# K, V, dV and dK moved one DMA per head pair in key order, and weights transposed on TensorE, in a two-block attention kernel with backward

## The chip, the cores and the metric

The kernel runs on one core of one Trainium2 chip. The metric is the device time of one execution in microseconds (us), lower is better. Durations below come from one profiled execution of the kernel before the change.

## What is computed

Two independent attention blocks A and B, each with its own x, caches and weights, run forward, and then the gradients of all ten inputs are computed from `grad_out`. For one block (the sizes are those of the inputs):

```python
B, Sq, D = 8, 96, 640          # batch, queries, model width
H, Sk, Dh = 32, 512, 128       # heads, keys, head width
q = (x @ wq).reshape(B, Sq, H, Dh).transpose(0, 2, 1, 3)
scores = einsum("bhqd,bhkd->bhqk", q, k_cache) * Dh ** -0.5
p = softmax(scores)
o = einsum("bhqk,bhkd->bhqd", p, v_cache)
out = o.transpose(0, 2, 1, 3).reshape(B, Sq, H * Dh) @ wo
...
_out, _vjp = jax.vjp(_f, A_x, A_k_cache, ..., B_wo)   # all inputs
_grads = _vjp(grad_out)
```

All arrays are bf16. Per block the outputs are `out`, dx, dK, dV, dwq and dwo. Per head and batch entry, K, V, dK and dV are 512x128 each, so 128 KB.

## The kernel before

**Ticks.** Work is cut into pieces that an `Emitter` sorts by (tick, slot). One tick is one (head, batch) pair: 2 blocks x 32 heads x 8 batch entries = 512 ticks. Heads go in pairs (`HP = 2`), and ticks alternate between the two heads of a pair for one batch entry. `OFF` and `HK` say by how many ticks a stage stands before or after its own tick; `SLOTS` sorts the stages inside a tick. The order of instructions on each engine follows from this table, and within what it leaves open from the framework's scheduler; engines run their own list in order and wait for each other by semaphores.

**The stages of one tick.** `c_s2a`: S = Q K^T (PE, tile `S_ps`) and the row maximum `negm` (DVE). `c_s2b`: exp into `E_sb` with row sums (ACT). `c_s3a`, `c_s3b`: 1/rowsum `rinv` (DVE) and P = E * rinv into `P_sb` (POOL). `c_s45`: P transposed on PE, copied by ACT to `PT_sb`; one tick later O^T from `V_sb` and `PT_sb` (tile `optp_ps`, copied to `OT_h`). `c_s4`: dV = P^T dO (`dV_ps`), copied by ACT to `dV_sb` (L325) and stored (L326). `c_s5b`, `c_s6`: `prod` on POOL, dP = dO V^T (`dP_ps`), the row term `dl_ps`, and dS = (dP - dl) * P on DVE into `dS_sb` (L349). `c_s78`: dS transposed and, a tick later, dQ^T from `K_sb`. `c_s7`: dK (`dK_ps`), copied by ACT to `dK_sb` (L389) and stored (L390).

**Loads.** `p_ldT` reads K and V of two heads transposed, by one transposing DMA each per head pair, into `KT_p` and `VT_p` (L232, 5 buffers). `c_ldn` reads K and V as they lie, one DMA per head, into `K_sb` and `V_sb` (L241, 7 buffers). All of these, the dV and dK stores and the transposed weight loads are issued from one queue, SP's (in the trace SPq). SP issues in order, and an issue that must wait holds everything behind it. `dV_sb` and `dK_sb` have 3 buffers each: ACT may write a buffer again only when the store from three heads earlier has landed.

**Key order.** In the transposed tile the key index is split as key = (r, f, c) with 8 x 16 x 4 values, and r lies innermost in memory. S reads it in the order (c, f, r), runs of 8 adjacent bf16. So the columns of S, P, dP and dS stand in that permuted order, and the natural loads and the dV, dK stores go through `keys_in`, which puts key (r, f, c) on partition (f, r).

**Per head.** `pA` loads the weights of a head pair (`wq_p` from POOL's queue, `woT_p` by a transposing DMA on SP, L172). `pC` makes Q^T and dO^T (tile `q_ps`), `pD` their untransposed forms, `qA`, `qB`, `qD` the weight gradients. After every group of 4 heads, `gW` loads `wo_r` and, transposed by a DMA on SP, `wqT_r` (L454), and 36 pieces `gU` (L477, tile `o_ps`) add the group's part to the output and to dx.

All PSUM tiles share 8 banks that go round in the order of the program.

Of the kernel before, what the change touches and what calls it, by code (L numbers as in the profile page):

```python
# [56 lines left out]
def build_block(tc, em, tick0, blk, x, kc, vc, wq, wo, g_all, out_all, dx, dk, dv, dwq, dwo, ident, ones, pools, HG=4, first=True, groups=None):  # L57
# [108 lines left out]
    def pA(h):  # L166
        def f():
            wq_p = hd.tile([128, DC, HP * 128], BF16, name="wq_p", bufs=2)
            with nc.allow_non_contiguous_dma(reason="per-pair wq slice"):
                nc.gpsimd.dma_start(wq_p[:], wq_v[:, :, h * 128:(h + HP) * 128])  # L170
            woT_p = hd.tile([128, DC, HP * 128], BF16, name="woT_p", bufs=2)
            nc.sync.dma_start_transpose(woT_p[:], wo[h * 128:(h + HP) * 128, :])  # L172
# [12 lines left out]

    def pC(h, which, si):
        def f():
            st = HS[(blk, h)]
            (t0, w) = tsplits[si]
            if which == 0:  # L190
                dst = st["QT_h"]
                lhs = lambda c: st["wq_h"][:, c, :]
                rhsT = S["xT"]
                sc = scale
            else:
                dst = st["dOT_h"]
                lhs = lambda c: st["woT_h"][:, c, :]
                rhsT = S["gT"]
                sc = None
            q_ps = bank([128, w], F32, "q_ps")  # L200
            for c in range(DC):
                nc.tensor.matmul(q_ps[:], lhs(c), rhsT[:, c, t0:t0 + w], start=(c == 0), stop=(c == DC - 1))  # L202
            evac(EV["pC%d%d" % (which, si)], dst[:, t0:t0 + w], q_ps[:], sc)
        return f
# [19 lines left out]
    def keys_in(kv, h, b):  # L224
        return kv[b, h].rearrange("(r f c) d -> f r (c d)", r=R8, f=F4, c=KC)

    def p_ldT(h, b, which):
        def f():
            key = "KT" if which == 0 else "VT"
            t_ = kvp.tile([128, F4 * KC, 16], BF16, name=key + "_p", bufs=5)  # L230
            src = (kc if which == 0 else vc)[b, h:h + HP].rearrange("h (r f) d -> (h r) (f d)", r=R8)
            nc.sync.dma_start_transpose(t_[:], src)  # L232
            for j in range(HP):
                CS.setdefault((blk, h + j, b), {})[key] = t_[:, :, j * R8:(j + 1) * R8].rearrange("p (f c) r -> p c f r", c=KC)
        return f

    def c_ldn(h, b, which):
        def f():
            key = "K_sb" if which == 0 else "V_sb"
            t_ = kvp.tile([128, KC, 128], BF16, name=key, bufs=7)  # L240
            nc.sync.dma_start(t_[:].rearrange("p c d -> p (c d)"), keys_in(kc if which == 0 else vc, h, b))  # L241
            CS[(blk, h, b)][key] = t_
        return f
# [72 lines left out]
    def c_s4(h, b):  # L316
        def f():
            st = CS[(blk, h, b)]
            hs = HS[(blk, h)]
            P_sb = st["P_sb"]  # L320
            dV_ps = bank([128, KC * 128], F32, "dV_ps")
            for c in range(KC):
                nc.tensor.matmul(dV_ps[:, c * 128:(c + 1) * 128], P_sb[:, c * 128:(c + 1) * 128], hs["dOnat_h"][:, b * 128:(b + 1) * 128], start=True, stop=True)  # L323
            dV_sb = wk.tile([128, KC * 128], BF16, name="dV_sb", bufs=3)
            nc.scalar.activation(dV_sb[:], dV_ps[:], ACT.Identity, scale=1.0)  # L325
            nc.sync.dma_start(keys_in(dv, h, b), dV_sb[:])  # L326
        return f
# [11 lines left out]
    def c_s6(h, b):  # L339
        def f():  # L340
            st = CS[(blk, h, b)]
            hs = HS[(blk, h)]
            tok = slice(b * Sq, (b + 1) * Sq)
            dP_ps = bank([Sq, Sk], F32, "dP_ps")
            nc.tensor.matmul(dP_ps[:], hs["dOT_h"][:, tok], st["VT"], start=True, stop=True)  # L345
            dl_ps = bank([Sq, 1], F32, "dl_ps")
            nc.tensor.matmul(dl_ps[:], st["prod"][:], ones[:, 0:1], start=True, stop=True)  # L347
            dS_sb = wk.tile([Sq, Sk], BF16, name="dS_sb", bufs=3)
            nc.vector.scalar_tensor_tensor(dS_sb[:], dP_ps[:], dl_ps[:, 0:1], st["P_sb"][:], op0=ALU.subtract, op1=ALU.mult)  # L349
            st["dS_sb"] = dS_sb  # L350
        return f

    def c_s78(k8, k7):
        def f():
# [23 lines left out]
        return f

    def c_s7(h, b):  # L380
        def f():
# [6 lines left out]
            dK_sb = wk.tile([128, KC * 128], BF16, name="dK_sb", bufs=3)  # L388
            nc.scalar.activation(dK_sb[:], dK_ps[:], ACT.Identity, scale=1.0)  # L389
            nc.sync.dma_start(keys_in(dk, h, b), dK_sb[:])  # L390
# [34 lines left out]
    def qD(h, c_lo, c_hi):  # L425
        def f():
            st = HS[(blk, h)]
            dQnat = st["dQnat"]
            pr = HS[(blk, h - h % HP)]
# [4 lines left out]
            j = h % HP  # L434
# [14 lines left out]
    def gW(g):  # L449
        def f():  # L450
            wo_r = grp.tile([128, HG, D], BF16, name="wo_r", bufs=1)
            nc.gpsimd.dma_start(wo_r[:, 0:groups[g], :], wo[GH0[g] * 128:(GH0[g] + groups[g]) * 128, :].rearrange("(h p) d -> p h d", p=128))
            wqT_r = grp.tile([128, HG, D], BF16, name="wqT_r", bufs=1)
            nc.sync.dma_start_transpose(wqT_r[:, 0:groups[g], :], wq[:, GH0[g] * 128:(GH0[g] + groups[g]) * 128])  # L454
            G[g] = dict(wo_r=wo_r, wqT_r=wqT_r)
# [39 lines left out]
    for g in range(NG):  # L495
        h0 = GH0[g]
        for hh in range(groups[g]):
# [12 lines left out]
            for b in range(B):  # L510
# [4 lines left out]
                em.add(ct + OFF["kn"], SLOTS["LOAD"], c_ldn(h, b, 0))  # L515
                em.add(ct + OFF["vn"], SLOTS["LOAD"], c_ldn(h, b, 1))
# [151 lines left out]
```

## Time and profile before

| | |
|---|---|
| device time, 2 runs | 2329.39 and 2347.51 us, median 2338.45 |
| the profiled execution | 2337.7 us, of which 2335.8 us are its span (first to last instruction) |
| granted TensorE clock, mean | 0.911 of full speed |
| busy share PE / DVE / ACT / POOL | 78 / 60 / 57 / 30 % |
| DMA | 479.49 MB in 419694 packets, 205 GB/s on average |
| HBM | 161.09 MB read, 159.12 MB written |

A span of 2335.8 us over 512 ticks is 4.56 us per tick. PE is TensorE's matmuls, PEld its weight loads, DVE VectorE, ACT ScalarE, POOL GpSimd, SP SyncE. Time in which an engine issues a DMA or waits is not counted as busy. Matmul rows overlap, so a matmul's duration is longer than the distance to the next one.

### The profile page before, as it was taken

To read this page: it belongs to the slowest core of one execution; us is meant where nothing else is said; L and a number is where in the kernel's file an instruction comes from. 1 tells how busy PE (TensorE), PEld (TensorE's weight loads), DVE (VectorE), ACT (ScalarE), POOL (GpSimd) and SP (SyncE) were. 2 spreads that over 40 slices of the span, in tenths; PEclk is the share of its full clock that TensorE was granted. 3 is DMA by queue.
4 is the path that set the end of the run, shared out by engine and by line. 5 is a ranking of instruction groups with operands and counts; after the bars stand their busy time and mean duration, and the time that the engine had idled before them with its cause. 6 is when DMAs were issued, how large, how long until landed. Compare 5 with 4: busy or idle time off the path is not lost.

```text
span 2335.8 us, 60652 instructions
## 1 busy us (share of the span) xinstructions
PE 1815.0 (78%) x22008; PEld 1447.8 (62%) x22008; DVE 1392.1 (60%) x3533; ACT 1342.1 (57%) x3465; POOL 690.4 (30%) x1258
## 2 busy tenths in 40 slices
PE   5777778787886877878877787777778787787887
PEld 3566666566665756656665565665656666575666
DVE  3554556565665656657665555655656656565665
ACT  3666655555565655655655576555565555555553
POOL 2222222222222322223344232222222223222225
PEclk8898998998999999889898999999998989989998
DMA  9777877878787877778888887887888878877774
GB/s 216 194 202 200 204 198 217 205 198 210 206 208 205 212 191 214 204 207 216 211 230 223 212 213 205 204 204 200 218 202 206 206 201 215 206 206 202 196 205 139
DMA packets 419694, 479.49 MB, mean 205 GB/s; under 512 B 136289, under 2 KB 399969, under 8 KB 411201
## 3 DMA queue, kind: packets, MB, share of 16 engines
q1 hardware_dynamic: 404512, 425.79, 71.9%
q0 software_dynamic: 14880, 49.82, 6.9%
q8 instruction: 172, 2.82, 0.5%
q14 instruction: 130, 1.06, 0.1%
HBM read 161.09 MB, written 159.12 MB: 137 GB/s over the span
## 4 chain that ended last, share of the span: by engine, by line
DMA 39%; PE 35%; ACT 13%; issue 5%; SPq 4%; DVE 3%; POOL 1%; ACTq 0%; POOLq 0%; DVEq 0%
DMA out_dram<-dK_sb 28%; DMA out_dram<-dV_sb 11%; PE q_ps L202 7%; ACT dK_sb L389 5%; PE o_ps L477 4%; PE S_ps L252 3%; ACT E_sb L264 3%; ACT dV_sb L325 3%; PE dwq_ps L440 2%; PE dwo_ps L418 2%; PE dK_ps L387 2%; PE dq_dst_ps L370 2%; PE dV_ps L323 2%; PE dq_dst_ps L363 2%; PE dP_ps L345 2%
## 5 line engine op out<-in xcount | busy, mean ns | idle before, releaser
L389 ACT ACTIVATE dK_sb<-dK_ps 128x512 bf16<-128x512 f32 x512 | 304.4, 594 | 590.2 <-DMA out_dram<-dK_sb 512.4
L283 POOL TENSOR_SCALAR P_sb<-E_sb,rinv 96x512 bf16<-96x512 bf16 x512 | 354.0, 691 | 741.4 <-DVE rinv L274 739.2
L254 DVE TENSOR_REDUCE negm<-S_ps 96x1 f32<-96x512 f32 x512 | 349.3, 682 | 216.7 <-PE S_ps L252 215.8
L264 ACT ACTIVATE E_sb<-S_ps,negm 96x512 bf16<-96x512 f32 x512 | 348.5, 681 | 135.3 <-DVE negm L254 129.6
L349 DVE SCALAR_TENSOR_TENSOR dS_sb<-dP_ps,dl_ps,P_sb 96x512 bf16<-96x512 f32 x512 | 382.3, 747 | 57.0 <-PE dl_ps L347 46.3
L325 ACT ACTIVATE dV_sb<-dV_ps 128x512 bf16<-128x512 f32 x512 | 307.1, 600 | 171.8 <-DMA out_dram<-dV_sb 125.2
L335 POOL TENSOR_TENSOR prod<-OT_h,dOT_h 128x96 bf16<-128x96 bf16 x512 | 187.6, 366 | 704.7 <-DVE OT_h L309 584.4
L252 PE MATMUL S_ps<-KT_p,QT_h 128*96 128x512 bf16 x512 | 213.1, 416 | 135.2 <-ACT dK_sb L389 117.0
L274 DVE RECIPROCAL rinv<-rowsum 96x1 f32<-96x1 f32 x512 | 80.7, 158 | 392.6 <-ACT E_sb L264 380.3
L312 ACT ACTIVATE PT_sb<-optp_ps 128x384 bf16<-128x384 bf16 x512 | 251.6, 491 | 1.7 <-DVE OT_h L309 0.6
L387 PE MATMUL dK_ps<-Qnat_h,dS_sb 96*128 96x128 bf16 x2048 | 216.0, 233 | 8.8 <-ACT dK_sb L389 5.7
L363 PE MATMUL dq_dst_ps<-dST_sb,K_sb 128*128 128x96 bf16 x2048 | 186.0, 218 | 39.9 <-ACT dK_sb L389 28.2
L323 PE MATMUL dV_ps<-dOnat_h,P_sb 96*128 96x128 bf16 x2048 | 213.3, 230 | 3.6 <-ACT dV_sb L325 3.3
L299 PE MATMUL optp_ps<-PT_sb,V_sb 128*128 128x96 bf16 x2048 | 185.2, 216 | 38.2 <-ACT PT_sb L312 22.9
L477 PE MATMUL o_ps<-wo_r,OT_h 128*128 128x256 bf16 (+1 forms) x1152 | 162.3, 265 | 66.8 <-ACT dK_sb L389 65.5
L345 PE MATMUL dP_ps<-VT_p,dOT_h 128*96 128x512 bf16 x512 | 209.5, 409 | 2.9 <-ACT dV_sb L325 2.3
L363 PEld LDWEIGHTS <-K_sb 128*128 128x128 bf16 x2048 | 148.9, 105 | 95.0 <-issue 78.6
L372 DVE COPY dST_sb<-dq_dst_ps 128x384 bf16<-128x384 bf16 x512 | 177.8, 347 | 47.0 <-PE dq_dst_ps L370 46.1
L370 PE MATMUL dq_dst_ps<-ident,dS_sb 96*128 96x96 bf16 x2048 | 187.1, 218 | 22.8 <-DVE dS_sb L349 22.5
L477 PE MATMUL o_ps<-wqT_r,dQT_h 128*128 128x256 bf16 (+1 forms) x1152 | 165.2, 267 | 45.7 <-ACT dK_sb L389 45.0
L202 PE MATMUL q_ps<-xT,wq_p 128*128 128x512 bf16 (+1 forms) x640 | 147.0, 359 | 63.3 <-ACT dK_sb L389 62.1
L306 PE MATMUL optp_ps<-ident,P_sb 96*128 96x96 bf16 x2048 | 184.3, 215 | 3.5 <-POOL P_sb L283 1.9
(71 smaller groups left out, 3343.1 us busy)
## 6 DMA issues: line engine op xcount, KB each, us to landing
out_dram<-dV_sb SPq DMA_DIRECT2D x512, 128.0 KB, 2.7
out_dram<-dK_sb SPq DMA_DIRECT2D x512, 128.0 KB, 2.7
V_sb<-in_A_v_cache_dram SPq DMA_DIRECT2D x256, 128.0 KB, 2.8
K_sb<-in_A_k_cache_dram SPq DMA_DIRECT2D x256, 128.0 KB, 2.9
V_sb<-in_B_v_cache_dram SPq DMA_DIRECT2D x256, 128.0 KB, 2.8
K_sb<-in_B_k_cache_dram SPq DMA_DIRECT2D x256, 128.0 KB, 2.8
out_dram<-dwo_sb POOLq DMA_DIRECT2D x64, 160.0 KB, 3.2
out_dram<-dwq_sb POOLq DMA_DIRECT2D x32, 320.0 KB, 4.9
```

What stands on the lines that cost most here:

```text
L202: nc.tensor.matmul(q_ps[:], lhs(c), rhsT[:, c, t0:t0 + w], start=(c == 0), stop=(c == DC - 1))
L252: nc.tensor.matmul(S_ps[:], hs["QT_h"][:, tok], st["KT"], start=True, stop=True)
L254: nc.vector.tensor_reduce(negm[:], S_ps[:], axis=AX.X, op=ALU.max, negate=True)
L264: nc.scalar.activation(E_sb[:], st["S_ps"][:], ACT.Exp, bias=st["negm"][:], scale=1.0, accum_out=rowsum[:])
L283: nc.gpsimd.tensor_scalar(P_sb[:], st["E_sb"][:], st["rinv"][:], 0.0, op0=ALU.mult, op1=ALU.add)
L323: nc.tensor.matmul(dV_ps[:, c * 128:(c + 1) * 128], P_sb[:, c * 128:(c + 1) * 128], hs["dOnat_h"][:, b * 128:(b + 1) * 128], start=True, s ...
L325: nc.scalar.activation(dV_sb[:], dV_ps[:], ACT.Identity, scale=1.0)
L349: nc.vector.scalar_tensor_tensor(dS_sb[:], dP_ps[:], dl_ps[:, 0:1], st["P_sb"][:], op0=ALU.subtract, op1=ALU.mult)
L363: nc.tensor.matmul(dQT_ps, st["K_sb"][:, c, :], st["dST_sb"][:, c * Sq:(c + 1) * Sq], start=(c == 0), stop=(c == KC - 1))
L387: nc.tensor.matmul(dK_ps[:, c * 128:(c + 1) * 128], dS_sb[:, c * 128:(c + 1) * 128], hs["Qnat_h"][:, b * 128:(b + 1) * 128], start=True, s ...
L389: nc.scalar.activation(dK_sb[:], dK_ps[:], ACT.Identity, scale=1.0)
L477: nc.tensor.matmul(o_ps[:], src[:, t * 128:(t + 1) * 128], rhs, start=(hh == 0), stop=(hh == groups[g] - 1))
```

## The change

1. **One DMA per head pair.** `p_ldn` replaces `c_ldn` and `p_st` replaces the two stores: each moves both heads of a pair, 256 KB. `K_sb`, `V_sb` then have 4 pair buffers instead of 7 single ones, `dK_sb` and `dV_sb` 2 pair buffers instead of 3 single ones, `KT_p` and `VT_p` 4 instead of 5.
2. **Key order.** The natural loads and the stores put keys 4p to 4p+3 on partition p. For that S reads `KT_p` in the order (c, r, f): its innermost step is 64 bf16 elements (128 bytes) and there are no runs of neighbours. dP reads `VT_p` in the order (f, c, r), runs of 8, and DVE reorders while it computes dS: it reads `dP_ps` with a step of 32 f32 elements and writes dS in S's order.
3. **Weights.** `pA` loads `wo_h` per head from POOL's queue. `pB` transposes it and `wq_p` on PE (5 + 5 transposes of 128x128 per head) and copies them out by ACT (`woT_h`) and DVE (`wqT_h`). The transposing DMAs of both weights go.
4. **Ticks and buffers.** `pA` and `pB` stand at other ticks; `OT_h` and `dQT_h` are allocated later; two pools lose one buffer each.

The core of the diff:

```diff
-    dict(pA=-12, pB=-12, pC0=[-6, -4], ...
-    dict(pA=-12, pB=-12, pC0=[-1, 3], ...
+    dict(pA=-10, pB=-7, pC0=[-6, -4], ...
+    dict(pA=-4, pB=-2, pC0=[-1, 3], ...
...
-            woT_p = hd.tile([128, DC, HP * 128], BF16, name="woT_p", bufs=2)
-            nc.sync.dma_start_transpose(woT_p[:], wo[h * 128:(h + HP) * 128, :])
+            wo_h = hd.tile([128, D], BF16, name="wo_h", bufs=1)
+            nc.gpsimd.dma_start(wo_h[:], wo[h * 128:(h + 1) * 128, :])
...
+            woT_ps = bank([128, DC * 128], BF16, "woT_ps")
+            for c in range(DC):
+                nc.tensor.transpose(woT_ps[:, c * 128:(c + 1) * 128], st["wo_h"][:, c * 128:(c + 1) * 128], ident[:])
+            woT_h = hd.tile([128, DC * 128], BF16, name="woT_h", bufs=1)
+            evac(EV["pB0"], woT_h[:], woT_ps[:])
...
+            wqT_ps = bank([128, DC * 128], BF16, "wqT_ps")
...
+            wqT_h = hst.tile([128, D], BF16, name="wqT_h")
+            evac(EV["pB1"], wqT_h[:], wqT_ps[:])
...
-            t_ = kvp.tile([128, F4 * KC, 16], BF16, name=key + "_p", bufs=5)
+            t_ = kvp.tile([128, F4 * KC, 16], BF16, name=key + "_p", bufs=4)
...
-                CS.setdefault((blk, h + j, b), {})[key] = t_[:, :, j * R8:(j + 1) * R8].rearrange("p (f c) r -> p c f r", c=KC)
+                half = t_[:, :, j * R8:(j + 1) * R8]
+                if which == 0:
+                    CS.setdefault((blk, h + j, b), {})[key] = half.rearrange("p (f c) r -> p c r f", c=KC)
+                else:
+                    CS.setdefault((blk, h + j, b), {})[key] = half.rearrange("p (f c) r -> p f c r", c=KC)
...
-            t_ = kvp.tile([128, KC, 128], BF16, name=key, bufs=7)
-            nc.sync.dma_start(t_[:].rearrange("p c d -> p (c d)"), keys_in(kc if which == 0 else vc, h, b))
+            t_ = kvp.tile([128, HP, KC, 128], BF16, name=key, bufs=4)
+            src = (kc if which == 0 else vc)[b, h:h + HP]
+            nc.sync.dma_start(t_[:].rearrange("p h c d -> p h (c d)"), src.rearrange("h (p c) d -> p h (c d)", c=KC))
...
+    def p_st(h, b, which):
+        def f():
+            t_ = CS[(blk, h, b)]["dV_p" if which == 1 else "dK_p"]
+            dst = (dv if which == 1 else dk)[b, h:h + HP]
+            nc.sync.dma_start(dst.rearrange("h (p c) d -> p h (c d)", c=KC), t_[:])
...
-            nc.vector.scalar_tensor_tensor(dS_sb[:], dP_ps[:], dl_ps[:, 0:1], st["P_sb"][:], op0=ALU.subtract, op1=ALU.mult)
+            nc.vector.scalar_tensor_tensor(dS_sb[:].rearrange("q (a f) -> q a f", f=F4), dP_ps[:].rearrange("q (f a) -> q a f", f=F4), dl_ps[:, 0:1],
+                                           st["P_sb"][:].rearrange("q (a f) -> q a f", f=F4), op0=ALU.subtract, op1=ALU.mult)
...
-            dK_sb = wk.tile([128, KC * 128], BF16, name="dK_sb", bufs=3)
-            nc.scalar.activation(dK_sb[:], dK_ps[:], ACT.Identity, scale=1.0)
-            nc.sync.dma_start(keys_in(dk, h, b), dK_sb[:])
+                st["dK_p"] = wk.tile([128, HP, KC * 128], BF16, name="dK_sb", bufs=2)
+            dK_p = CS[(blk, h - j, b)]["dK_p"]
+            nc.scalar.activation(dK_p[:, j], dK_ps[:], ACT.Identity, scale=1.0)
...
-            nc.sync.dma_start_transpose(wqT_r[:, 0:groups[g], :], wq[:, GH0[g] * 128:(GH0[g] + groups[g]) * 128])
...
-                em.add(ct + OFF["kn"], SLOTS["LOAD"], c_ldn(h, b, 0))
-                em.add(ct + OFF["vn"], SLOTS["LOAD"], c_ldn(h, b, 1))
+                    em.add(ct + OFF["kn"], SLOTS["LOAD"], p_ldn(h, b, 0))
+                    em.add(ct + OFF["vn"], SLOTS["LOAD"], p_ldn(h, b, 1))
+                    em.add(ct + HP + OFF["s4"], SLOTS["LOAD"], p_st(h, b, 1))
+                    em.add(ct + HP + OFF["s7"] + 1, SLOTS["LOAD"], p_st(h, b, 0))
```

How this moves the instructions. SP's list before, somewhere in the steady part of block A: these ten rows are what one head pair needs for one batch entry, two ticks (the shapes of the stores are those on the DRAM side, 16 x 8 rows of 512 elements).

```order
L232 DMA_TRANSPOSE KT_p_15561<-in_A_k_cache_dram 128x64x16
L241 DMA K_sb_15563<-in_A_k_cache_dram 128x1x512
L241 DMA V_sb_15559<-in_A_v_cache_dram 128x1x512
L390 DMA out_2_dram<-dK_sb_15398 16x8x512
L326 DMA out_3_dram<-dV_sb_15418 16x8x512
L241 DMA K_sb_15636<-in_A_k_cache_dram 128x1x512
L241 DMA V_sb_15640<-in_A_v_cache_dram 128x1x512
L232 DMA_TRANSPOSE VT_p_15638<-in_A_v_cache_dram 128x64x16
L390 DMA out_2_dram<-dK_sb_15492 16x8x512
L326 DMA out_3_dram<-dV_sb_15512 16x8x512
```

SP's list of the changed kernel for the same two ticks' worth of work:

```order
L242 DMA_TRANSPOSE VT_p_16950<-in_A_v_cache_dram 128x64x16
L265 DMA out_3_dram<-dV_sb_16900 128x2x512
L242 DMA_TRANSPOSE KT_p_17051<-in_A_k_cache_dram 128x64x16
L256 DMA V_sb_17229<-in_A_v_cache_dram 128x2x512
L265 DMA out_2_dram<-dK_sb_16976 128x2x512
L256 DMA K_sb_17330<-in_A_k_cache_dram 128x2x512
```

Ten issues have become six: the transposing loads are the same, and eight transfers of 128 KB are four of 256 KB. Each of the four loads waits for the last PE instruction that reads the buffer it refills (dP, S, O^T and dQ^T of the same two ticks), each store for the ACT copy just before it.

PE's list of the changed kernel where a head's weights are transposed; ahead of these rows stand four more transposes of `wo_h`, behind them the dwo matmuls of an older head.

```order
L185 LDWEIGHTS wo_h
L185 MATMUL woT_ps<-ident,wo_h 128x128
L191 LDWEIGHTS wq_p
L191 MATMUL wqT_ps<-ident,wq_p 128x128
L191 LDWEIGHTS wq_p
L191 MATMUL wqT_ps<-ident,wq_p 128x128
L191 LDWEIGHTS wq_p
L191 MATMUL wqT_ps<-ident,wq_p 128x128
L191 LDWEIGHTS wq_p
L191 MATMUL wqT_ps<-ident,wq_p 128x128
L191 LDWEIGHTS wq_p
L191 MATMUL wqT_ps<-ident,wq_p 128x128
```

These ten transposes and their weight loads per head are new on PE; nothing of the kind stood there before. On POOL's list one issue of `wo_h` per head is new, each placed right behind the transposes that free the tile's one buffer.

More of the change, by code (lines that the diff above doesn't have):

```diff
@@ L167, in f @@
         def f():
-            wq_p = hd.tile([128, DC, HP * 128], BF16, name="wq_p", bufs=2)
-            with nc.allow_non_contiguous_dma(reason="per-pair wq slice"):
-                nc.gpsimd.dma_start(wq_p[:], wq_v[:, :, h * 128:(h + HP) * 128])
-            woT_p = hd.tile([128, DC, HP * 128], BF16, name="woT_p", bufs=2)
-            nc.sync.dma_start_transpose(woT_p[:], wo[h * 128:(h + HP) * 128, :])
-            for j in range(HP):
-                HS[(blk, h + j)] = dict(woT_h=woT_p[:, :, j * 128:(j + 1) * 128], wq_h=wq_p[:, :, j * 128:(j + 1) * 128])
+            wo_h = hd.tile([128, D], BF16, name="wo_h", bufs=1)
+            nc.gpsimd.dma_start(wo_h[:], wo[h * 128:(h + 1) * 128, :])
+            j = h % HP
+            if j == 0:
+                wq_p = hd.tile([128, DC, HP * 128], BF16, name="wq_p", bufs=2)
+                with nc.allow_non_contiguous_dma(reason="per-pair wq slice"):
+                    nc.gpsimd.dma_start(wq_p[:], wq_v[:, :, h * 128:(h + HP) * 128])
+            else:
+                wq_p = HS[(blk, h - j)]["wq_p"]
+            HS[(blk, h)] = dict(wo_h=wo_h, wq_p=wq_p, wq_h=wq_p[:, :, j * 128:(j + 1) * 128])
         return f
@@ L428, in f @@
             dQnat = st["dQnat"]
[L429 removed]
+            j = h % HP
+            pr = HS[(blk, h - j)]
             if "dwq_sb" not in pr:
```

57 lines of the change are left out of this document (35 added, 22 removed).

## The prediction, made before the changed kernel was run

> **What bounds the kernel now.** I read the page first: engine shares, DMA queues, the chain of work that ended last.
>
> ```profile
> PE 1815.0 (78%) x22008; PEld 1447.8 (62%) x22008; DVE 1392.1 (60%) x3533; ACT 1342.1 (57%) x3465; POOL 690.4 (30%) x1258
> DMA packets 419694, 479.49 MB, mean 205 GB/s; under 512 B 136289, under 2 KB 399969, under 8 KB 411201
> q1 hardware_dynamic: 404512, 425.79, 71.9%
> q0 software_dynamic: 14880, 49.82, 6.9%
> DMA 39%; PE 35%; ACT 13%; issue 5%; SPq 4%; DVE 3%; POOL 1%; ACTq 0%; POOLq 0%; DVEq 0%
> DMA out_dram<-dK_sb 28%; DMA out_dram<-dV_sb 11%; PE q_ps L202 7%; ACT dK_sb L389 5%; PE o_ps L477 4%; PE S_ps L252 3%; ACT E_sb L264 3%; ACT dV_sb L325 3%; PE dwq_ps L440 2%; PE dwo_ps L418 2%; PE dK_ps L387 2%; PE dq_dst_ps L370 2%; PE dV_ps L323 2%; PE dq_dst_ps L363 2%; PE dP_ps L345 2%
> ```
>
> No engine is full, and 39% of the chain is the two stores. The waits, then who waits for the tile `dK_sb`, show how a store holds up PE:
>
> ```profile
> ACT dK_sb L389 <- DMA out_dram<-dK_sb: 512.4, 270, 6.8
> ACT dV_sb L325 <- DMA out_dram<-dV_sb: 125.2, 115, 8.3
> ```
>
> ```profile
>   PE S_ps L252: 118.7, 63
>   PE o_ps L477: 110.5, 77
>   PE q_ps L202: 65.7, 26
>   PE nat_ps L403: 28.5, 15
>   PE dq_dst_ps L363: 28.2, 19
> ```
>
> ACT stands 637.6 us before copies whose target buffer is still being stored. The PSUM bank of the waiting copy is not freed, and PE, which takes banks in order, stands behind it: 351.6 us in these five rows alone. Why the stores are late is seen on SP's queue (rows of the timeline; the last column of an ACT row is its wait):
>
> ```profile
> 999.62 0.60 ACT L389 ACTIVATE dK_sb<-dK_ps 128x512 bf16<-128x512 f32 x1 [4.68 <-DMA out_dram<-dK_sb]
> ...
> 1003.78 0.59 SPq L241 DMA_DIRECT2D K_sb<-in_A_k_cache_dram  x1
> 1004.47 0.58 SPq L241 DMA_DIRECT2D V_sb<-in_A_v_cache_dram  x1
> 1005.13 0.59 SPq L390 DMA_DIRECT2D out_dram<-dK_sb  x1
> 1005.82 1.18 SPq L232 DMA_TRANSPOSE VT_p<-in_A_v_cache_dram  x1
> 1007.09 0.58 SPq L326 DMA_DIRECT2D out_dram<-dV_sb  x1
> 1007.76 0.59 SPq L241 DMA_DIRECT2D K_sb<-in_A_k_cache_dram  x1
> ...
> 1009.11 0.59 SPq L390 DMA_DIRECT2D out_dram<-dK_sb  x1
> ...
> 1013.27 0.60 ACT L389 ACTIVATE dK_sb<-dK_ps 128x512 bf16<-128x512 f32 x1 [2.93 <-DMA out_dram<-dK_sb]
> ```
>
> ```profile
> 1009.11 4.08 DMA out_dram<-dK_sb
> ```
>
> SP issues without a pause: an issue of 128 KB takes 0.58 us, the next begins 0.09 us later. With three buffers, the copy at 1013.27 (the third `dK_sb` copy after the one at 999.62) reuses that one's buffer; its store was issued only at 1009.11, nine us after the data were ready, and by the chain took 4.08 us. **SP's issue rate is the bound.** Its ledger, by medians:
>
> ```profile
> L390 SPq DMA_DIRECT2D out_dram<-dK_sb x512: 537/591/1737, 52.7 to 2305.9; - x171
> L241 SPq DMA_DIRECT2D V_sb<-in_A_v_cache_dram x256: 536/577/2212, 20.0 to 1147.2; - x128
> L232 SPq DMA_TRANSPOSE KT_p<-in_A_k_cache_dram x128: 1115/1223/5842, 11.6 to 1122.3; - x128
> L172 SPq DMA_TRANSPOSE woT_p<-in_A_wo_dram x16: 1408/1876/9679, 1.8 to 955.7; - x16
> L454 SPq DMA_TRANSPOSE wqT_r<-in_A_wq_dram x8: 2867/3444/4700, 48.2 to 1126.7; - x8
> ```
>
> 2048 direct issues x 0.67 = 1372; 512 transposes x 1.30 (1.18 to 1.22, and 0.09) = 666; 32 x 1.97 and 16 x 3.53 for the weights = 120. Together 2158 of 2336 us; the rows above their medians fill most of the rest.
>
> **The change, part by part.**
>
> *SP.* 1024 direct issues and the 120 us of weights go. Left: 1024 of twice the size and 512 transposes. What does an issue of 256 KB cost? Two rows:
>
> ```profile
> 0.74 0.46 SPq L139 DMA_DIRECT2D x_nat<-in_A_x_dram  x1
> x_nat<-in_A_x_dram SPq DMA_DIRECT2D x1, 960.0 KB, 5.2
> ```
>
> A direct DMA of 960 KB was issued in 0.46 us, so the cost does not go with the size; but the queue was empty then, and the transposes do get dearer with size. The ends are 0.58 and 1.16 us; I take 0.58, the nearer row. SP then needs 1024 x 0.67 + 666 = 1352 us (or 1946 with the upper end). Per pair and batch entry that is 5.3 us instead of 8.0, over two ticks that now last 9.1. The stores are no longer late: a pair's store follows its second copy at once, and its buffer is written again only three ticks later, some 11 us at 3.8 us per tick, against 4.1 us of landing and at most 5.3 us of issues ahead of it. So I count the ACT waits for stores as gone. The price of the new order is that `KT_p` and `VT_p`, with 4 buffers, are refilled as soon as PE has read the old content, so an SP issue can stand waiting for PE, and stores stand behind it; the three ticks cover that as well.
>
> *What is late next: PE.* Its pace where no store is in the way is seen in four stretches (us; busy time and matmul count of PE, ..., granted clock, DMA share, GB/s):
>
> ```profile
> 511.70:531.00 19.30, 19.30 (x277) 16.50 (x274) 15.76 (x44) 12.96 (x35) 7.85 (x14) 1.00 0.81 218
> 1799.60:1819.90 20.30, 19.64 (x251) 16.14 (x250) 14.28 (x40) 13.08 (x35) 6.75 (x12) 0.92 0.88 215
> 2079.70:2105.70 26.00, 25.33 (x313) 20.32 (x313) 18.61 (x50) 17.33 (x46) 9.27 (x16) 0.90 0.87 223
> 2224.90:2244.30 19.40, 19.40 (x277) 16.58 (x275) 15.73 (x44) 13.07 (x35) 6.92 (x13) 1.00 0.74 198
> ```
>
> 1118 matmuls in 85.0 us, 76.0 ns each; all 22008 at that pace are 1673 us. That is an estimate, since the mix of shapes differs from stretch to stretch.
>
> *What PE, ACT, DVE and POOL get.* The rows, from the groups, the timeline and the chain:
>
> ```profile
> 1008.33 0.55 PE L217 MATMUL n_ps<-ident,QT_h 128*96 128x128 bf16 x7
> L312 ACT ACTIVATE PT_sb<-optp_ps 128x384 bf16<-128x384 bf16 x512 | 251.6, 491 | 1.7 <-DVE OT_h L309 0.6 <-PE optp_ps L306 0.5
> L422 POOL DMA_DIRECT2D out_dram<-dwo_sb x64 | 38.5, 601 | 57.5 <-ACT dwo_sb L159 45.4 <-ACT dx_acc L159 5.7 <-ACT out_acc L159 3.9
> L349 DVE SCALAR_TENSOR_TENSOR dS_sb<-dP_ps,dl_ps,P_sb 96x512 bf16<-96x512 f32 x512 | 382.3, 747 | 57.0 <-PE dl_ps L347 46.3 <-POOL prod L335 3.4 <-PE n_ps L217 1.7
> L254 DVE TENSOR_REDUCE negm<-S_ps 96x1 f32<-96x512 f32 x512 | 349.3, 682 | 216.7 <-PE S_ps L252 215.8
> 1016.91 0.22 PE S_ps L252
> ```
>
> Transposes: 640 x 0.55/7 = 50 us on PE. Their copies, 640 columns: at most 491 x 640/384 = 0.82 us, 64 times, so 52 us on ACT and as much on DVE, which end at 1395 and 1444 us, both hidden under PE. The `wo_h` issues: 64 x 0.60 = 39 us on POOL, which is 30% busy; behind one stand `P_sb` and `prod` for 0.6 us, an eighth of a tick. Without cover this would be 143 us more on the path.
>
> dS reads `dP_ps` with a step of 128 bytes. No row shows such a read; between 0.75 us as now and twice that, DVE ends between 1444 and 1827 us. It stays below PE either way, so I add nothing and keep the upper end for the range.
>
> S is the open term. It reads single elements 128 bytes apart, where it read runs of 8. In the chain an S of 512 columns takes 0.22 us with its 64 runs, 3.4 ns per run. Ends: nothing, or 3.4 ns for every single element, 1.74 us per S, 778 us in all. The slowest reader of single elements among the rows is DVE's reduction, 682/512 = 1.33 ns; PE at that rate would need 0.68 us, 236 us in all. I take half of PE's present rate, 0.43 us, **+110 us**: nearer to the rows, which show no loss, than to the far end, but not at zero, as no row reads without runs.
>
> The Trainium skill, page "SBUF — State Buffer", section "Door 1: The DMA port swizzle", says that SBUF reads go by lines of 16 bytes and keep the full rate only with two hits or more per line, so that bf16 may be strided by up to 8 elements for free. The row of S today, whose runs of 8 are just such a line, agrees; the page speaks against the new read, gives no price, and by it the sum has a term above zero here, without it none.
>
> *Sum.* 1673 + 50 + 110 = 1833 us at the stretches' pace. PE's idle time now is 2335.8 - 1815.0 = 521 us; less the 351.6 us of the five rows, 169 are left, part of which the dV stores cause. I keep 100 of them, by choice. 1833 + 100 = 1933, with 1.9 us outside the span (2337.7 against 2335.8) about **1930 us**. The profiled execution stands 0.75 us below the median of the runs, so nothing is corrected for that.
>
> **The rivals.**
>
> *The strided read is free.* 1933 - 110: 1820 us. For it: runs of 8 cost nothing today. Against it: see above.
>
> *The transfers become the bound.* DMA is now busy for 78.8% of 2336, 1841 us per engine. The transposed weights (32 x 328 KB + 16 x 655 KB = 21 MB) go and 10.5 MB of `wo_h` come: by bytes 1841 x 469/479.5 = 1801 us. At 1930 that is 93%, more than any of the four stretches had (0.74 to 0.88). If 0.88 is the ceiling, 2050 us; if 256 KB also cost 1.16 us of issue, SP's 1946 plus PE's waits for late loads give about 2080. Take 2070.
>
> *The waits stay under another name.* If the refills waiting for PE held the stores by more than the three ticks, ACT would wait as now: some 2310 us. Against it: each refill waits for PE work of the same two ticks, and the stores have three.
>
> *Slower: S becomes the bound.* At 3.4 ns per element S takes 1.74 us: 1820 + 778 = 2600 us. It decides from (2338 - 1820)/512 = 1.0 us more per S, 2.4 ns per element, which is nearly twice DVE's 1.33 ns. That speaks against it.
>
> **How the numbers follow.** Forecast (1860 to 2010, around 1930): 0.46. Free read (1780 to 1860): 0.18. Transfers or SP, or dS at twice its time (2010 to 2180): 0.22. Waits stay (2290 to 2338): 0.06. Slower: 0.08. The range is 1780 to 2180 and leaves out 0.14 and some tails. About 2% is what a measurement of this kernel can tell from no change: below 2291 lie the first three, 0.86; within 2% the fourth, 0.06; above, 0.08.
>
> **What would show it.** The pair issues on SPq near 0.58 us (the SP rival: 1.16). ACT's wait for `dK_sb` stores below 50 us instead of 512.4. An S in the chain at 0.43 us instead of 0.22 (free: 0.22; slower: above 1.2). dS still near 747 ns. The granted clock above 0.911, since long idle times of PE go. DMA share near 0.9. The prediction is wrong if PE is again idle by more than 20%, or if the chain has a store at its head.

## The result, and the profile after

| | before | after |
|---|---|---|
| device time, median of 2 runs | 2338.45 us | 2016.19 us (2013.47 and 2018.91) |
| ratio to before, with its 95% interval | | 0.8622 [0.847, 0.8774] |
| span of the profiled execution | 2335.8 us | 2011.7 us |
| granted TensorE clock | 0.911 | 0.991 |

The change took 322 us off. The forecast was 1930 us with a range of 1780 to 2180; the time lies in the range, 86 us above the forecast, and 6 us above the band that belonged to the forecast's own mechanism (1860 to 2010). The page of the changed kernel, in the same parts as before (busy time, slices, queue, chain):

```profile
PE 1957.6 (97%) x22648; PEld 1370.4 (68%) x22648; DVE 1439.6 (72%) x3597; ACT 1359.0 (68%) x3529; POOL 723.5 (36%) x1322
PEclk9999999999999999999999999999999999999999
DMA  8998989988889888888889989888898989979883
DMA packets 322913, 468.88 MB, mean 233 GB/s; under 512 B 37472, under 2 KB 301152, under 8 KB 314432
q1 hardware_dynamic: 304672, 404.75, 77.2%
PE 91%; DMA 3%; issue 2%; DVE 2%; POOL 1%; ACT 1%; POOLq 0%; SPq 0%; DVEq 0%; ACTq 0%
PE S_ps L285 21%; PE q_ps L215 10%; PE o_ps L512 9%; PE dV_ps L356 5%; PE dK_ps L422 5%; PE dP_ps L380 5%; PE dwq_ps L477 5%; PE dwo_ps L455 5%; PE dq_dst_ps L406 4%; PE optp_ps L339 4%; PE optp_ps L332 4%; PE dq_dst_ps L399 4%; PE n_ps L230 3%; PE nat_ps L440 2%; DMA out_dram<-ob 1%
```

The chain was 39% stores and is now 91% PE; PE is busy 97% of the span at nearly the full clock. What ended ACT's idle time before the `dK_sb` copies (rows of that tile), ACT's wait for `dV_sb` stores, and the longest of the waits that PE ends:

```profile
  PE dK_ps L422: 111.2, 119
  DMA out_dram<-dK_sb: 0.8, 1
```

```profile
ACT dV_sb L361 <- DMA out_dram<-dV_sb: 1.2, 2, 0.7
DVE negm L287 <- PE S_ps L285: 256.5, 485, 4.0
```

ACT's 512.4 us of waits for `dK_sb` stores are 0.8 us, the 125.2 us for `dV_sb` stores 1.2 us. But DVE now waits 485 times for S, 256.5 us in all (before 221 times, 215.8 us). The groups and three steps of the chain show why:

```profile
L285 PE MATMUL S_ps<-KT_p,QT_h 128*96 128x512 bf16 x512 | 521.8, 1019 | 2.6 <-DVE ob L523 1.2
L380 PE MATMUL dP_ps<-VT_p,dOT_h 128*96 128x512 bf16 x512 | 196.9, 385 | 0.0
L384 DVE SCALAR_TENSOR_TENSOR dS_sb<-dP_ps,dl_ps,P_sb 96x512 bf16<-96x512 f32 x512 | 383.0, 748 | 50.7 <-PE dl_ps L382 37.6
L191 PE MATMUL wqT_ps<-ident,wq_p 128*128 128x128 bf16 x320 | 31.9, 223 | 0.2 <-ACT E_sb L297 0.2
L185 PE MATMUL woT_ps<-ident,wo_h 128*128 128x128 bf16 x320 | 29.4, 224 | 1.0 <-ACT dK_sb L427 0.8 <-DMA wo_h<-in_A_wo_dram 0.2
```

```profile
1002.33 0.22 PE dP_ps L380
...
1002.79 0.86 PE S_ps L285
1003.65 1.08 PE dwo_ps L455 x5
```

S and dP have the same shape. dP, which reads runs of 8, still takes 0.22 us on the chain; S, which reads single elements 128 bytes apart, takes 0.86 us. (From its own start to the next matmul's start it is 0.84 us in the median of all 512.) In busy time S costs 521.8 - 196.9 = 325 us more than dP in the same kernel. dS, which reads PSUM with a step of 128 bytes, has the 748 ns of before (747). SP's rows (minimum, median, maximum in ns) and its longest wait:

```profile
L256 SPq DMA_DIRECT2D V_sb<-in_A_v_cache_dram x128: 372/526/1888, 14.8 to 973.6; - x128
L256 SPq DMA_DIRECT2D K_sb<-in_A_k_cache_dram x128: 367/374/1626, 19.6 to 983.5; - x128
L265 SPq DMA_DIRECT2D out_dram<-dK_sb x256: 372/419/2301, 42.7 to 1982.5; - x128
```

```profile
SPq L256 <- PE dK_ps L422: 371.5, 205, 3.4
```

An issue of 256 KB is cheaper than one of 128 KB was (0.37 to 0.53 against 0.58 us), and SP now waits for PE. Summed over all its issue rows, with the 0.09 us behind each, SP was occupied for 2295 of 2336 us before and is for 1340 of 2012 us now.

### The profile page after: what moved, and what is told of

The parts are those of the page before. It is cut to its first block, busy times and chain, and to the rows that moved or that the text cites. A ratio compares the mean times of both kernels' runs of the same rounds, so it can differ in the third digit from the quotient of the medians.

```text
span 2011.7 us, 59742 instructions
## 1 busy us (share of the span) xinstructions
PE 1957.6 (97%) x22648; PEld 1370.4 (68%) x22648; DVE 1439.6 (72%) x3597; ACT 1359.0 (68%) x3529; POOL 723.5 (36%) x1322
## 4 chain that ended last, share of the span: by engine, by line
PE 91%; DMA 3%; issue 2%; DVE 2%; POOL 1%; ACT 1%; POOLq 0%; SPq 0%; DVEq 0%; ACTq 0%
PE S_ps L285 21%; PE q_ps L215 10%; PE o_ps L512 9%; PE dV_ps L356 5%; PE dK_ps L422 5%; PE dP_ps L380 5%; PE dwq_ps L477 5%; PE dwo_ps L455 5%; PE dq_dst_ps L406 4%; PE optp_ps L339 4%; PE optp_ps L332 4%; PE dq_dst_ps L399 4%; PE n_ps L230 3%; PE nat_ps L440 2%; DMA out_dram<-ob 1%
## 5 line engine op out<-in xcount | busy, mean ns | idle before, releaser
L287 DVE TENSOR_REDUCE negm<-S_ps 96x1 f32<-96x512 f32 x512 | 351.3, 686 | 257.8 <-PE S_ps L285 256.5
L285 PE MATMUL S_ps<-KT_p,QT_h 128*96 128x512 bf16 x512 | 521.8, 1019 | 2.6 <-DVE ob L523 1.2
L356 PE MATMUL dV_ps<-dOnat_h,P_sb 96*128 96x128 bf16 x2048 | 199.6, 220 | 0.0
L422 PE MATMUL dK_ps<-Qnat_h,dS_sb 96*128 96x128 bf16 x2048 | 199.4, 220 | 0.0
L380 PE MATMUL dP_ps<-VT_p,dOT_h 128*96 128x512 bf16 x512 | 196.9, 385 | 0.0
L406 PE MATMUL dq_dst_ps<-ident,dS_sb 96*128 96x96 bf16 x2048 | 173.2, 207 | 16.4 <-DVE dS_sb L384 16.4
L512 PEld LDWEIGHTS <-OT_h 128*128 128x128 bf16 x1152 | 101.4, 99 | 118.7 <-issue 104.1
L512 PEld LDWEIGHTS <-dQT_h 128*128 128x128 bf16 x1152 | 102.3, 99 | 115.9 <-issue 97.5
L399 PE MATMUL dq_dst_ps<-dST_sb,K_sb 128*128 128x96 bf16 x2048 | 171.7, 207 | 0.0
L477 PEld LDWEIGHTS <-x_nat 128*128 128x128 bf16 x1920 | 120.8, 98 | 58.2 <-issue 46.6
L399 PEld LDWEIGHTS <-K_sb 128*128 128x128 bf16 x2048 | 134.2, 98 | 35.2 <-issue 16.7
```

The lines of the kernel that those rows point to most:

```text
L285: nc.tensor.matmul(S_ps[:], hs["QT_h"][:, tok], st["KT"], start=True, stop=True)
L287: nc.vector.tensor_reduce(negm[:], S_ps[:], axis=AX.X, op=ALU.max, negate=True)
L399: nc.tensor.matmul(dQT_ps, st["K_sb"][:, c, :], st["dST_sb"][:, c * Sq:(c + 1) * Sq], start=(c == 0), stop=(c == KC - 1))
L422: nc.tensor.matmul(dK_ps[:, c * 128:(c + 1) * 128], dS_sb[:, c * 128:(c + 1) * 128], hs["Qnat_h"][:, b * 128:(b + 1) * 128], start=True, s ...
L512: nc.tensor.matmul(o_ps[:], src[:, t * 128:(t + 1) * 128], rhs, start=(hh == 0), stop=(hh == groups[g] - 1))
```

## The experiments

The theory after the result: before, SP's issue rate was the bound; the change lifted it and made PE the bound, with the strided read of S as PE's largest new item. Rivals: the DMA engines, busy for 87% of the span, bind; or SP, whose refills now wait for PE, binds; or the gain comes from one part alone. Ratios are to the kernel before, timed on the same chip beside each run; 2353.19 us in the first four, 2348.4 us in the others.

**1. S reads runs of 8, exp puts the columns in order** (the changed kernel otherwise).

```diff
-                if which == 0:
-                    CS.setdefault((blk, h + j, b), {})[key] = half.rearrange("p (f c) r -> p c r f", c=KC)
-                else:
-                    CS.setdefault((blk, h + j, b), {})[key] = half.rearrange("p (f c) r -> p f c r", c=KC)
+                CS.setdefault((blk, h + j, b), {})[key] = half.rearrange("p (f c) r -> p f c r", c=KC)
...
-                nc.scalar.activation(E_sb[:], st["S_ps"][:], ACT.Exp,
+                nc.scalar.activation(E_sb[:].rearrange("q (a f) -> q a f", f=F4), st["S_ps"][:].rearrange("q (f a) -> q a f", f=F4), ACT.Exp,
```

> The changed kernel, but S reads K^T as dP reads V^T, in runs of 8 neighbours, and the exp on ACT puts the columns in key order while it reads S from PSUM (step of 32 f32). Theory (the single-element read of S, 0.84 us from one start to the next instead of 0.22, fills PE): S falls back to 0.22 us, PE loses 0.62 x 512 = 320 us of work, and the time falls until the next engine binds; the DMA engines are busy for 87% of 2012 us = 1750 us, so about 1790 us (1720 to 1850). ACT's exp stays near 0.68 us, as dS stayed at 748 ns with the same kind of read. Rival (the DMA engines bind at 87%): at least 1960 us. Rival (SP's refills that wait for PE bind): at least 1960 us. If ACT pays for the strided PSUM read, its exp row goes above 0.75 us.

Measured: 1806.57 us, ratio 0.7687 [0.7662, 0.7711]. Its page and two groups:

```profile
PE 1669.4 (92%) x22648; PEld 1379.5 (76%) x22648; DVE 1396.3 (77%) x3597; ACT 1349.9 (75%) x3529; POOL 723.7 (40%) x1322
DMA  9999999999999999999999999999999999999993
q1 hardware_dynamic: 304672, 404.75, 86.1%
q0 software_dynamic: 17952, 60.31, 10.3%
L294 ACT ACTIVATE E_sb<-S_ps,negm 96x512 bf16<-96x512 f32 x512 | 348.5, 681 | 215.7 <-DVE negm L284 208.4
L282 PE MATMUL S_ps<-KT_p,QT_h 128*96 128x512 bf16 x512 | 197.3, 385 | 5.0 <-DVE ob L520 1.8
```

S is back at dP's size, PE has 288 us less to do, and the exp takes 681 ns with the stepped PSUM read (680 in the changed kernel). The strided read alone costs this kernel some 210 us. Both rivals are out as the bound at 2016 us; at 1807 us the DMA engines are busy for 97% (86.1 + 10.3 and the instruction queues), PE for 92%, and SP's issues fill 1645 of 1812 us. Which of them binds there this run doesn't show.

**2. The strided read alone, in the kernel before.**

```diff
-                ... t_[:, :, j * R8:(j + 1) * R8].rearrange("p (f c) r -> p c f r", c=KC)
+                ... t_[:, :, j * R8:(j + 1) * R8].rearrange("p (f c) r -> p c r f" if which == 0 else "p (f c) r -> p c f r", c=KC)
```

> The kernel before with one edit: S reads K^T in single elements 128 bytes apart, as the changed kernel does (the key order of S then no longer agrees with the natural loads; only the time is read). Theory (SP's issue rate bound the kernel before, and PE had idle time): most of the 320 us that S costs more falls into PE's idle time of 521 us, so 2340 to 2440 us, I take 2380. Rival (PE's work was on the path all along): 2338 + 320 = 2660 us.

Measured: 2345.83 us, ratio 0.9979 [0.9956, 1.0003]. S among the groups, and ACT's longest wait for a store:

```profile
L252 PE MATMUL S_ps<-KT_p,QT_h 128*96 128x512 bf16 x512 | 523.1, 1022 | 83.8 <-ACT dK_sb L389 77.6 <-ACT dV_sb L325 2.6 <-ACT E_sb L264 1.9
```

```profile
ACT dK_sb L389 <- DMA out_dram<-dK_sb: 343.1, 183, 4.6
```

S costs as much here as in the changed kernel, and the time does not move at all: ACT's wait for `dK_sb` stores shrinks from 512.4 to 343.1 us instead. So PE's work did not bind before; SP's queue did: its issues, with 0.09 us behind each, fill 2301 of 2342 us here, as they filled 2295 of 2336 before. I had expected some 40 us to show.

**3. The changed kernel with two issues per pair.**

```diff
-            nc.sync.dma_start(t_[:].rearrange("p h c d -> p h (c d)"), src.rearrange("h (p c) d -> p h (c d)", c=KC))
+            for j in range(HP):
+                nc.sync.dma_start(t_[:, j].rearrange("p c d -> p (c d)"), src[j].rearrange("(p c) d -> p (c d)", c=KC))
...
-            nc.sync.dma_start(dst.rearrange("h (p c) d -> p h (c d)", c=KC), t_[:])
+            for j in range(HP):
+                nc.sync.dma_start(dst[j].rearrange("(p c) d -> p (c d)", c=KC), t_[:, j])
```

> The changed kernel, same tiles, order and buffers, but every pair DMA is issued as two DMAs of 128 KB, one per head. Theory (what the pairs saved is SP's issue time): 1024 more issues, SP's ledger 2048 x 0.67 + 666 = 2038 us plus its waits for PE, so SP is full again and the time rises to 2100 to 2300 us, I take 2180. Rival (the gain came from the stores' place in the order, from the key order or from the weights): 2000 to 2050 us, no change beyond 2%.

Measured: 2022.47 us, ratio 0.861 [0.8586, 0.8634]; the changed kernel had 0.8622. My theory failed here: without pairs the time is the same.

```profile
PE 1958.5 (97%) x22648; PEld 1370.9 (68%) x22648; DVE 1439.7 (71%) x3597; ACT 1357.3 (67%) x3529; POOL 723.5 (36%) x1322
L257 SPq DMA_DIRECT2D V_sb<-in_A_v_cache_dram x256: 334/434/1812, 14.5 to 979.9; - x128
L267 SPq DMA_DIRECT2D out_dram<-dK_sb x512: 332/387/2118, 37.3 to 1988.3; - x171
```

An issue of 128 KB takes 0.39 to 0.43 us here, not 0.58. Its size is that of before and its addresses are not, so the key order is the likely cause; run 6 tests it. SP is then just fast enough to stay behind a PE that is 97% busy: its issues fill 1936 of 2017 us.

**4. The changed kernel with weights transposed by DMA again.** `pB`'s transposes and copies go.

```diff
-            wo_h = hd.tile([128, D], BF16, name="wo_h", bufs=1)
-            nc.gpsimd.dma_start(wo_h[:], wo[h * 128:(h + 1) * 128, :])
+                woT_p = hd.tile([128, DC, HP * 128], BF16, name="woT_p", bufs=2)
+                nc.sync.dma_start_transpose(woT_p[:], wo[h * 128:(h + HP) * 128, :])
...
+            wqT_r = grp.tile([128, HG, D], BF16, name="wqT_r", bufs=1)
+            nc.sync.dma_start_transpose(wqT_r[:, 0:groups[g], :], wq[:, GH0[g] * 128:(GH0[g] + groups[g]) * 128])
```

> The changed kernel with the weights transposed by DMA again (the transposing loads on SP, no transposes and no copies of weights on PE, ACT and DVE). Theory (PE is the bound): PE loses 640 x 0.06 = 38 us and SP, which has some 700 us of waits, takes the 120 us of issues: 1970 to 2000 us, I take 1985. Rival (DMA is the bound; 21 MB of small packets come back): 2060 us or more. Rival (a transposing issue of 2 to 3.4 us holds a store): 2030 to 2080 us.

Measured: 1992.68 us, ratio 0.8487 [0.8463, 0.8511].

```profile
PE 1930.7 (97%) x22008; PEld 1342.7 (67%) x22008; DVE 1409.6 (71%) x3533; ACT 1318.4 (66%) x3465; POOL 687.3 (34%) x1258
DMA packets 403291, 479.28 MB, mean 240 GB/s; under 512 B 119904, under 2 KB 383584, under 8 KB 394816
```

The sign is that of the theory: PE loses 27 us where I expected 38, and the time about as much. In this kernel, with PE as the bound, the third part of the change costs about 1%. The changed kernel was timed on another occasion, and the intervals of the two ratios overlap, so PE's 27 us are the firmer number. The part takes 10.4 MB off the DMA engines, which are not yet the bound.

**5. What a read of S costs, by its steps.** One kernel, eight ways to read `KT_p`, by batch entry:

```diff
-                nc.tensor.matmul(S_ps[:], hs["QT_h"][:, tok], st["KT"], start=True, stop=True)
+                nc.tensor.matmul(S_ps[:], hs["QT_h"][:, tok], st["KTV"][b], start=True, stop=True)
...
+                        half.rearrange("p (f c) r -> p c r f", c=KC),
+                        half.rearrange("p (f c) r -> p r c f", c=KC),
+                        half.rearrange("p g r -> p r g"),
+                        half.rearrange("p g (a e) -> p a g e", e=2),
+                        half.rearrange("p g (a e) -> p a g e", e=4),
+                        half.rearrange("p g (e a) -> p a g e", e=4),
+                        half.rearrange("p g (e a) -> p a g e", e=2),
+                        half.rearrange("p g r -> p g r"),
```

> The changed kernel, but S reads K^T in eight ways, one for each batch entry (the columns of S then stand in other orders than the rest; only the duration of S is read): b=0 and 1 single elements 128 bytes apart, b=2 single elements 32 bytes apart, b=3 runs of 2 neighbours, b=4 runs of 4, b=5 four elements 4 bytes apart and then the next 32 bytes, b=6 two elements 8 bytes apart and then the next 32 bytes, b=7 runs of 8. Theory (each visit of a new 16-byte line costs a fixed time, 0.84/512 = 1.64 ns, hidden while a line gives enough elements): 0.84 us for b=0, 1, 2; 0.42 us for b=3 and 6; 0.22 us for b=4, 5, 7. Rival by the page SBUF of the Trainium skill (two hits on a line are enough): 0.22 us for b=3 and 6 as well. Rival (only neighbours count): b=5 and 6 at 0.84 us.

Measured: 1864.53 us in a single run; only S is read from it. The timeline of one head pair, one S row for each two ticks, b = 0 to 7 (start, duration in us); for b = 0 and 3 the next row of PE stands below:

```profile
919.60 1.02 PE L295 MATMUL S_ps<-KT_p,QT_h 128*96 128x512 bf16 x1
920.44 0.80 PE L487 MATMUL dwq_ps<-dQnat,x_nat 128*128 128x128 bf16 x11
...
926.90 1.04 PE L295 MATMUL S_ps<-KT_p,QT_h 128*96 128x512 bf16 x1
...
933.86 1.08 PE L295 MATMUL S_ps<-KT_p,QT_h 128*96 128x512 bf16 x1
...
941.73 0.62 PE L295 MATMUL S_ps<-KT_p,QT_h 128*96 128x512 bf16 x1
942.16 0.35 PE L522 MATMUL o_ps<-wo_r,OT_h 128*128 128x128 bf16 x3
...
949.88 0.39 PE L295 MATMUL S_ps<-KT_p,QT_h 128*96 128x512 bf16 x1
...
958.55 0.39 PE L295 MATMUL S_ps<-KT_p,QT_h 128*96 128x512 bf16 x1
...
965.15 0.62 PE L295 MATMUL S_ps<-KT_p,QT_h 128*96 128x512 bf16 x1
...
971.74 0.38 PE L295 MATMUL S_ps<-KT_p,QT_h 128*96 128x512 bf16 x1
```

A row is longer than the distance to the next start (1.02 us against 0.84, 0.38 against 0.22), and that distance is what a read costs. In the median of the 64 reads of each form, single elements cost 0.84 to 0.90 us, two elements per 16 bytes 0.44 us, four 0.23 us, eight 0.22 us. Whether the two or four are neighbours makes no difference (b = 3 and 6, b = 4 and 5), so both rivals are out. The cost goes by visits of a new line, some 1.6 to 1.8 ns each (0.84/512, 0.44/256, 0.23/128), as long as that is more than the columns take. A new line always lies at least 32 bytes on in these reads, so they can't tell lines of 16 bytes from longer ones; and why single elements 32 bytes apart (0.90 us) cost more than those 128 bytes apart (0.84 us) is not shown. The rule of the Trainium skill, page "SBUF — State Buffer", section "Door 1: The DMA port swizzle", that two hits per line keep the full rate, does not hold for this read: two hits give half the rate, four nearly the full one.

**6. Key order alone, in the kernel before.** One DMA per head, weights by DMA, buffers and ticks as before; S reads runs of 8, exp and dS reorder.

```diff
-        return kv[b, h].rearrange("(r f c) d -> f r (c d)", r=R8, f=F4, c=KC)
+        return kv[b, h].rearrange("(p c) d -> p (c d)", c=KC)
...
-                CS.setdefault(...)[key] = t_[:, :, j * R8:(j + 1) * R8].rearrange("p (f c) r -> p c f r", c=KC)
+                CS.setdefault(...)[key] = t_[:, :, j * R8:(j + 1) * R8].rearrange("p (f c) r -> p f c r", c=KC)
```

and the exp of experiment 1 with the dS of the changed kernel.

> The kernel before with key order alone: one DMA per head as before, weights by DMA as before, same buffers and ticks, but natural loads and stores put keys 4p to 4p+3 on partition p; S reads K^T in runs of 8, exp and dS put the columns in key order while they read PSUM. Theory (key order makes a direct issue cheaper: 0.39 to 0.53 us in the run with single issues against 0.58 before, so SP's ledger falls by about 2048 x 0.12 = 250 us, and SP still binds): about 2090 us (2030 to 2150). Rival (an issue costs what it cost; only fewer issues help): 2340 us, no change.

Measured: 2066.97 us, ratio 0.8804 [0.8777, 0.8832].

```profile
L241 SPq DMA_DIRECT2D V_sb<-in_A_v_cache_dram x256: 334/403/2199, 19.5 to 1007.9; - x128
L241 SPq DMA_DIRECT2D K_sb<-in_A_k_cache_dram x256: 339/424/1588, 25.0 to 1017.9; - x128
```

```profile
ACT dK_sb L390 <- DMA out_dram<-dK_sb: 266.5, 156, 5.7
```

With the same number of DMAs of the same size, key order alone takes 12% off: a natural load is issued in 0.40 to 0.42 us instead of 0.58. All issues of SP together take 1766 us instead of 2060, and the span is 276 us shorter. SP still binds: with 0.09 us behind each its issues fill 2001 of 2059 us, and ACT waits 266.5 us for `dK_sb` stores.

**7. Experiment 1 with two issues per pair** (the edit of experiment 3 on top of it).

```diff
+                nc.sync.dma_start(t_[:, j].rearrange("p c d -> p (c d)"), src[j].rearrange("(p c) d -> p (c d)", c=KC))
...
+                nc.sync.dma_start(dst[j].rearrange("(p c) d -> p (c d)", c=KC), t_[:, j])
```

> The run in which exp reorders (1807 us), with every pair DMA issued as two, one per head. Theory (there the DMA engines bind, 97% busy; SP's ledger with single issues is 2048 x 0.54 + 666 = 1770 us, just under it): 1810 to 1870 us, I take 1840. Rival (with PE out of the way SP binds again without pairs): above 1900 us.

Measured: 1971.44 us, ratio 0.8401 [0.8377, 0.8425]. The rival was right: once S no longer fills PE, pairs are worth some 165 us.

```profile
PE 1721.1 (87%) x22648; PEld 1402.0 (71%) x22648; DVE 1402.2 (71%) x3597; ACT 1358.8 (69%) x3529; POOL 723.5 (37%) x1322
ACT dV_sb L360 <- DMA out_dram<-dV_sb: 68.8, 44, 3.8
ACT dK_sb L426 <- DMA out_dram<-dK_sb: 62.9, 54, 4.5
```

All issue rows of SP, with 0.09 us behind each, add up to 1906 of 1967 us: SP binds again. My ledger of 1770 us went by medians; the rows above them made the difference.

Against run 6, SP's issues fall from 2001 to 1906 us and the time from 2067 to 1971. What the two differ in is mainly the transposing weight loads, which are off SP here; ticks and buffers differ too and were not tried alone. So where SP binds, the third part of the change is worth up to some 95 us, though it costs about 1% where PE binds.

**8. Experiment 1 with wo loaded once.** The output pieces `gU` read `wo_h`, kept in the 8 buffers of its pool, and `wo_r` goes (one buffer less for `ld_tmp`, for room).

```diff
-            wo_h = hd.tile([128, D], BF16, name="wo_h", bufs=1)
+            wo_h = hst.tile([128, D], BF16, name="wo_h")
...
-            nc.gpsimd.dma_start(wo_r[:, 0:groups[g], :], wo[GH0[g] * 128:(GH0[g] + groups[g]) * 128, :].rearrange("(h p) d -> p h d", p=128))
...
-                rhs = G[g]["wo_r"][:, hh, c0:c0 + w] if which == 0 else HS[(blk, h)]["wqT_h"][:, c0:c0 + w]
+                rhs = HS[(blk, h)]["wo_h"][:, c0:c0 + w] if which == 0 else HS[(blk, h)]["wqT_h"][:, c0:c0 + w]
```

> The run in which exp reorders (1807 us), with wo loaded once: the output pieces read wo_h, kept in 8 buffers, instead of wo_r, so 10.5 of 469 MB go. Theory (the DMA engines bind): 1807 x 458/469 = 1767 us, 1755 to 1785. Rival (PE, 92% busy, or the chain between the engines binds): 1795 to 1810 us.

Measured: 1788.2 us, ratio 0.7614 [0.7583, 0.7645]. It got faster by 1% where 2.2% of the bytes went, which lies between the two expectations. So the DMA engines are at most a part of what binds at 1807 us; and `ld_tmp` has a buffer less here, which was not tried alone.

```profile
PE 1659.0 (93%) x22648; PEld 1374.9 (77%) x22648; DVE 1392.6 (78%) x3597; ACT 1346.6 (75%) x3529; POOL 710.1 (40%) x1306
DMA packets 320610, 458.39 MB, mean 257 GB/s; under 512 B 37217, under 2 KB 300897, under 8 KB 312129
```

This is the fastest version of the study, 11% under the changed kernel's time.

## Why the prediction was right, and where its terms were off

**What bound the kernel before: right.** The run with S strided in the kernel before leaves the time where it was, though S's busy time grows by 310 us (213.1 to 523.1); the run with key order alone shows that cheaper issues shorten it. Where SP binds, the span stays within some 60 us of what its issues fill:

| kernel | SP's issues, 0.09 us behind each (us) | span (us) |
|---|---|---|
| before | 2295 | 2336 |
| S strided in it (run 2) | 2301 | 2342 |
| key order alone (run 6) | 2001 | 2059 |
| run 1 with two issues per pair (run 7) | 1906 | 1967 |
| changed kernel | 1340 | 2012 |

**SP's new ledger: right in sum, wrong in what it rests on.** I counted 1352 us with 0.58 us per pair issue. All issue rows after, with 0.09 us each, add up to 1340 us. That the sums agree is luck: the direct issues were cheaper than I took (0.37 to 0.53 us, 596 us in all with what follows each, against 686), the transposing ones dearer by nearly as much (743 against 666). And I had put the whole saving on the number of DMAs. I never asked what the new addresses do to the cost of an issue. Runs 3, 6 and 7 show both: key order saves enough for a PE-bound kernel, pairs count once PE is out of the way.

**The stores' slack: right.** 512.4 us of waits became 0.8, 125.2 became 1.2; SP's refills do wait for PE (371.5 us in one row), at no cost to the stores.

**The strided read of S: the mis-sized term.** This is the step that failed: I took half of PE's rate, 110 us; S runs at a quarter of the rate and costs 325 us. The far end (3.4 ns per element, 778 us) was too high, since the run of 8 is limited by its columns and not by its line: in run 5 a visit costs some 1.7 ns. DVE's 1.33 ns lay nearer than the value I chose, but by coincidence, as it is DVE's pace for neighbouring columns and says nothing of TensorE's read. No row had a size. The page "SBUF — State Buffer" of the Trainium skill had the right sign.

**PE's pace and idle time: too high by some 150 us, which hid two thirds of that error.** That was luck: with these two terms as they turned out and S at 110, the sum would have been 1572 + 50 + 110 + 54 = 1786 us, 226 below the 2012 measured. The terms beside what they turned out to be, in PE's busy time:

| term | forecast | measured |
|---|---|---|
| the matmuls of before, S at dP's price | 1673 | 1957.6 - 325 - 61 = 1572 |
| transposes of weights | 50 | 31.9 + 29.4 = 61 |
| S strided | 110 | 325 |
| idle | 100 | 2011.7 - 1957.6 = 54 |
| sum | 1933 | 2012 |

The four stretches had granted clocks of 0.90 to 1.00; with PE never idle for long the whole kernel runs at 0.991, at 1572/22008 = 71.4 ns per matmul where I took 76.0. The two stretches with clock 1.00 alone would have given 38.7/554 = 69.9 ns.

**dS, ACT, DVE, POOL: right.** dS 748 ns, no wait worth naming; ACT and DVE stay under PE.

**The rivals.** "Free read" was refuted by the S row; run 1 shows what it would have been worth, 1807 us against the 1820 I gave. The path is another, though: I counted on a kernel that PE fills but for 100 us, and run 1 has PE busy for 1669 us and the DMA engines for 97%. "Transfers bind" was wrong at 2016 us: its ceiling of 0.88 is not one, as run 1 reaches 0.97. At 1807 us it is at most true in part (run 8). The time of 2016 us lies in the band that I gave to transfers, SP or a dS of twice its time (2010 to 2180), and none of these bound the kernel: PE did, by S. The slower one is out: 0.86 us per S, below the 1.2 us from which it decides.

## What to carry to other kernels

Read an issuing queue like an engine: if its issues follow each other without a pause, it is the first suspect for the bound (in run 3 it was nearly full and PE bound), and both the number of DMAs and the way their addresses run decide its time. When a bound is lifted, work that was free before is paid in full: the strided read cost nothing in the kernel before and 210 us in the changed one. Put a reordering where it is free: here ScalarE's and VectorE's reads from PSUM, not TensorE's read from SBUF.

## What the runs showed of the hardware beyond what I expected

- TensorE's moving read from SBUF pays per line visited, some 1.7 ns: one bf16 element per visit gives a quarter of the rate (0.84 us for 512 columns), two in 16 bytes half (0.44), four nearly the full rate (0.23), eight the full one (0.22).
- ACT's exp and DVE's dS read f32 from PSUM with a step of 128 bytes at their usual pace: 681 against 680 ns and 748 against 747 ns.
- A direct DMA's issue on SP gets little dearer with its size (0.38 to 0.43 us for 128 KB, 0.37 to 0.53 us for 256 KB, both in order), more so with its pattern: 0.58 us for 128 KB spread as 16 x 8 rows in DRAM. Whether the further dimension of the pattern or the spread addresses cause it was not tried.
- One kind of issue stretched as the DMA engines filled up. In the four kernels with the changed kernel's order on SP, the transposing load of K took 1.13, 1.80, 2.12 and 2.26 us in the median at a DMA share of 87% (changed), 94% (run 5), 96% (run 8) and 97% (run 1); that of V stayed at 1.11 to 1.18 us. In runs 6 and 7, in another order, K's took 1.11 and 1.12 us at 91 to 92%. What sets K's load apart is not shown. Block A's rows of run 1 and of the changed kernel:

```profile
L242 SPq DMA_TRANSPOSE KT_p<-in_A_k_cache_dram x128: 1102/2270/8126, 1.8 to 862.4; - x128
```

```profile
L242 SPq DMA_TRANSPOSE KT_p<-in_A_k_cache_dram x128: 1095/1144/7989, 1.8 to 964.1; - x128
```
